# An expert layer's second product turned from channels on partitions to tokens on partitions

## The chip, the cores and the metric

The program runs on one core of a Trainium2 chip, as one launch. The metric is the device time of one execution in microseconds, the median of several runs. A core has five engines that run side by side, each with its own in-order instruction stream: TensorE (PE, with its weight loads shown apart as PEld), VectorE (DVE), ScalarE (ACT), GpSimd (POOL) and SyncE (SP), which in this kernel issues all the DMAs. They wait for one another through semaphores.

## The reference

Three layers follow one another: a linear attention, a mixture of four experts in which every token goes through all four, and a gated feed-forward layer. Only the middle one is touched by the change. With 2304 tokens, 512 channels, four experts and 1024 hidden units each:

```python
p = domain_probs / (domain_probs.sum(-1, keepdims=True) + 1e-09)   # (2304, 4)
out = np.zeros((N, D))
for e in range(E):
    h = np.maximum(x @ w1[e], 0.0)          # (2304, 1024)
    out += p[:, e:e + 1] * (h @ w2[e])      # (2304, 512)
```

The layer after it computes `((x @ w1) * (x @ w2)) @ w3 @ w_out`. All is in float32.

## The kernel before, in words

**Tiling.** The tokens are cut into six blocks j of 384 (TB). The hidden units are cut into quarters of 256, so the experts have 16 chunks c (four experts, four quarters each); the last layer has four chunks more. `visits` lists which chunk is computed for which blocks: the first visits, on the early blocks, run while the attention of later heads is still going on; the last visit (number 22, chunk 15) goes over all six blocks.

**Precision.** A float32 value x is written as hi + lo, where hi is rounded to a format that TensorE reads in one pass (F32R). A product is then three matmuls, hi·hi, hi·lo and lo·hi (`PASSES`). Some of the attention's matmuls (kvp, num and P of some head pairs) take plain float32 operands; each of them appears in the trace as two records.

**One step (visit v, block j) of the experts.** `up` (L655) makes two PSUM tiles [128 hidden units, 384 tokens], 12 matmuls each. For each of the two, DVE applies relu and multiplies by the token's share of this expert (L738; the share is the tile pb, a row of pT in DRAM broadcast over 128 partitions by a DMA, L669), ACT rounds the result to h's hi half (L741), and DVE subtracts to get the lo half (L743). One step later `down1` (L689) multiplies h by the second weight w_b. It puts channels on the partitions: for each of four groups d of 128 channels, w_b is the stationary operand, h the moving one, 384 columns wide, six matmuls. DVE adds the result to the block's running sum acc (L697 copies for the first chunk, L700 adds). At chunk 15 DVE adds into PSUM (L705), and the sum, which has its channels on partitions as the next layer wants it, is rounded and split straight into that layer's input x (L708 on ACT, L710 on DVE).

**Shares.** `load_probs` (L367 to L381) loads the 4 × 2304 shares as pn in runs of 18 floats, normalizes them on DVE, and stores them to pT.

**Order.** Nothing is written in program order. The body of the kernel lists operations with a length and a priority; `Prog.run` simulates a list scheduler with these lengths and emits each engine's instructions in the order that it finds. Expert steps have a base priority of EXPERTS·n; the tables AHEAD and KLEAD set where the attention's 16 head pairs stand among them. So a change of one operation's length, or of which engine it needs, can move instructions anywhere behind it. The PSUM pool mma has three buffers and serves `down1`; mmb has five and serves `up` once the attention is over.

**Start.** GpSimd fills the two vx tiles with constants (L826, L827) and then runs partition_all_reduce on the attention's q side (tile M from Ps, L504), 64 times. DVE subtracts M from Ps (L507), ACT takes exponentials of it (Eq, L512), and PE multiplies (num, L528). DVE, ACT and PE also work on the k side (P, mx, E, kvp).

## Time and profile before

| | us |
|---|---|
| median of three runs | 1367.98 (1367.87 to 1369.09) |
| the profiled execution, own time | 1359.98 |
| its span (first to last instruction) | 1358.2 |
| PE busy | 1336.0 (98%) |
| DVE busy | 882.3 (65%) |
| ACT busy | 439.1 (32%) |
| POOL busy | 88.5 (7%) |

The profiled execution took 1.8 us more than its span, and 8.0 us less than the median of the runs without a profile. A difference worked out inside the span is carried to the median as it is. The span has two stages: the attention, mixed with the first expert steps, up to 294 us (where the last num matmul starts), and after that the experts and the last layer alone.

In the views, busy time counts an instruction from its start to its modelled end; matmuls overlap one another, so that the pace of a row of matmuls is read from the distance between two starts, and not from the duration of one.

### The profile page before, as it was taken

The page shows a single profiled execution, that of the slowest core. Times are in us where ns is not written, and L with a number is a line of the kernel's source. Part 1 is how long each engine was busy: PE and PEld are TensorE (multiplying, and loading weights), DVE is VectorE, ACT ScalarE, POOL GpSimd, SP SyncE. Part 2 cuts the span into 40 slices and gives each one's busy share as a digit, 9 for nine tenths or more (in the row PEclk, how much of TensorE's full clock was granted, in tenths as well). Part 3 has the DMA queues.
Part 4 walks back from the last instruction along what each step waited for, and adds up shares of the span by engine and source line. Part 5 has one row for each costly group of instructions (what it writes and reads, how often), then busy time and mean ns, then how long its engine had stood idle before and what let it go on. Part 6 is the DMA issues. An engine that isn't in the chain of part 4 may idle for free.

```text
span 1358.2 us, 19233 instructions
## 1 busy us (share of the span) xinstructions
PE 1336.0 (98%) x7691; PEld 1288.8 (95%) x7691; DVE 882.3 (65%) x1553; ACT 439.1 (32%) x935; POOL 88.5 (7%) x72
## 2 busy tenths in 40 slices
PE   8899999999999999999999999999999999999998
PEld 7779989999999999999999999999999999999998
DVE  6778998888986655656656566565578737353333
ACT  6777775862322111112112121121134312121111
POOL 3333321310000000000000000000000000000000
PEclk9989999999999999999999999999999999999999
DMA  5463332223321102122021021110010202000012
GB/s 151 132 183 106 89 108 76 71 58 111 114 97 56 47 1 70 38 63 76 2 69 39 32 88 49 39 57 21 24 47 32 78 1 70 1 0 1 1 47 93
DMA packets 59640, 82.86 MB, mean 61 GB/s; under 512 B 30336, under 2 KB 33792, under 8 KB 56992
## 3 DMA queue, kind: packets, MB, share of 16 engines
q1 hardware_dynamic: 59552, 81.64, 19.7%
q8 instruction: 60, 0.98, 0.3%
q14 instruction: 28, 0.23, 0.1%
HBM read 74.63 MB, written 7.00 MB: 60 GB/s over the span
## 4 chain that ended last, share of the span: by engine, by line
PE 91%; DVE 4%; DMA 2%; ACT 2%; issue 1%; SPq 0%
PE dn L689 28%; PE up L655 28%; PE upva L655 7%; PE upvb L655 7%; PE dnv L792 7%; PE kvp L441 5%; PE psw L588 3%; PE num L528 2%; DMA d<-den 1%; PE P L414 1%; DMA den<-xq 1%; ACT E L433 1%; ACT Eq L512 0%; DVE Ps L507 0%; DVE rb L557 0%
## 5 line engine op out<-in xcount | busy, mean ns | idle before, releaser
L689 PE MATMUL dn<-h,w_b 128*128 128x384 f32 x2304 | 424.1, 335 | 1.8 <-DVE acc L697 0.9
L655 PE MATMUL up<-x,w_a 128*128 128x384 f32 x2304 | 420.3, 334 | 0.0
L689 PEld LDWEIGHTS dn<-h,w_b 128*128 128x128 f32 x2304 | 401.1, 188 | 6.5 <-DVE h L743 1.5
L655 PEld LDWEIGHTS up<-x,w_a 128*128 128x128 f32 x2304 | 401.3, 188 | 2.9
L700 DVE TENSOR_TENSOR acc<-dn,acc 128x384 f32<-128x384 f32 x336 | 185.2, 555 | 106.2 <-PE dn L689 105.1
L741 ACT CAST h<-up 128x384 fp32r<-128x384 f32 x192 | 92.1, 480 | 471.0 <-DVE up L738 467.6
L738 DVE SCALAR_TENSOR_TENSOR up<-up,pb 128x384 f32<-128x384 f32 x192 | 108.2, 563 | 110.4 <-PE up L655 109.3
L743 DVE TENSOR_TENSOR h<-up,h 128x384 fp32r<-128x384 f32 x192 | 105.5, 551 | 37.8 <-ACT h L741 37.6
L655 PE MATMUL upva<-x,w_va 128*128 128x384 f32 x576 | 108.8, 336 | 0.0
L655 PE MATMUL upvb<-x,w_vb 128*128 128x384 f32 x576 | 107.8, 336 | 0.0
L655 PEld LDWEIGHTS upva<-x,w_va 128*128 128x128 f32 x576 | 102.0, 188 | 1.7
L792 PE MATMUL dnv<-w_vo,gs 128*128 128x512 f32 x432 | 102.5, 391 | 0.0
L655 PEld LDWEIGHTS upvb<-x,w_vb 128*128 128x128 f32 x576 | 100.5, 188 | 0.0
L768 DVE TENSOR_TENSOR g<-upvb,a 128x384 f32<-128x384 f32 x48 | 26.7, 556 | 112.9 <-PE upvb L655 112.9
L504 POOL PARTITION_ALL_REDUCE M<-Ps x64 | 86.7, 1356 | 197.6 <-ACT Ps L501 187.3
L792 PEld LDWEIGHTS dnv<-w_vo,gs 128*128 128x128 f32 x432 | 80.9, 188 | 15.9
L441 PEld LDWEIGHTS kvp<-vx,E 128*128 128x128 f32 x640 | 78.6, 193 | 3.6 <-ACT E L433 1.1
L441 PE MATMUL kvp<-vx,E 128*128 128x66 f32 x640 | 78.0, 273 | 0.9 <-ACT E L433 0.8
L528 PE MATMUL num<-Eq,KV 128*128 128x288 f32 x328 | 69.9, 343 | 7.7 <-ACT Eq L512 4.0
L528 PEld LDWEIGHTS num<-Eq,KV 128*128 128x128 f32 x328 | 50.9, 190 | 15.6 <-ACT Eq L512 5.3
L763 ACT COPY a<-upva 128x384 f32<-128x384 f32 x48 | 23.0, 480 | 123.7 <-PE upva L655 123.7
L588 PE MATMUL psw<-w_f,w_f 128*128 128x512 f32 x192 | 54.6, 393 | 0.0
(92 smaller groups left out, 1055.7 us busy)
## 6 DMA issues: line engine op xcount, KB each, us to landing
raw_a<-w SPq DMA_DIRECT2D x42, 256.0 KB
raw_b<-w SPq DMA_DIRECT2D x42, 256.0 KB
qr<-qT SPq DMA_DIRECT2D x32, 288.0 KB
cr_f<-w3T SPq DMA_DIRECT2D x8, 1024.0 KB
vx<-vt SPq DMA_DIRECT2D x16, 320.0 KB
kr<-kT SPq DMA_DIRECT2D x15, 320.0 KB
rb<-rd SPq DMA_DIRECT2D x32, 144.0 KB
pb<-pT SPq DMA_DIRECT2D x24, 192.0 KB
```

The costliest lines, as they stand in the source:

```text
L441: nc.tensor.matmul(kvp()[:, a, h], E()[:, t, a, h], w()[:, t0 + t, h], start=t0 + t == 0 and h == 0 and a == 0, stop=t0 + t == 4, skip_gro ...
L504: op(POOL, 1171, lambda M=M, Ps=Ps: nc.gpsimd.partition_all_reduce(M(), Ps(), channels=128, reduce_op=bass_isa.ReduceOp.absmax), reads=[Ps ...
L528: nc.tensor.matmul(num(), KV[i]()[:, a, 2 * h:2 * h + 2].rearrange("p c d -> p (c d)"), EE[j]()[:, a], start=n == 0, stop=n == len(parts) - 1)
L588: nc.tensor.matmul(ps(), w3[fc]()[:, a, gc * 128:(gc + 1) * 128], wo[gc // 2]()[:, b, gc % 2 * DM:(gc % 2 + 1) * DM], start=gc == 0 and n ...
L655: nc.tensor.matmul(ps(), w()[:, a, kk * QF + fc * 128:kk * QF + (fc + 1) * 128], xs[b]()[:, kk], start=kk == 0 and n == 0, stop=kk == 3 an ...
L689: nc.tensor.matmul(ps(), w()[:, x, fc * DM + d * 128:fc * DM + (d + 1) * 128], hs[fc]()[:, y], start=fc == 0 and n == 0, stop=fc == 1 and ...
L700: op(DVE, dve(TB), lambda ps=ps, part=part: nc.vector.tensor_tensor(out=part(), in0=ps(), in1=part(), op=ALU.add), reads=[ps], writes=[a])
L738: op(DVE, dve(TB), lambda ps=ps, s=s: nc.vector.scalar_tensor_tensor(out=ps(), in0=ps(), scalar=0.0, in1=s(), op0=ALU.max, op1=ALU.mult), ...
L741: op(ACT, act(TB, False), lambda ps=ps, h=h: nc.scalar.copy(out=h()[:, 0], in_=ps()), reads=[ps], fills=[h])
L743: op(DVE, dve(TB), lambda ps=ps, h=h: nc.vector.tensor_tensor(out=h()[:, 1], in0=ps(), in1=h()[:, 0].bitcast(F32), op=ALU.subtract), reads ...
L768: op(DVE, dve(TB), lambda a=a, pb=pb, g=g: nc.vector.tensor_tensor(out=g(), in0=pb(), in1=a(), op=ALU.mult), reads=[a, pb], writes=[g])
L792: nc.tensor.matmul(ps(), gs[fc]()[:, a, t * 128:(t + 1) * 128], w()[:, b, fc * DM:(fc + 1) * DM], start=fc == 0 and n == 0, stop=fc == 1 a ...
```

## The change

- `down1` puts tokens on the partitions: for each of three groups t of 128 tokens, h is the stationary operand and w_b the moving one, 512 columns wide, six matmuls. Per step that is 18 matmuls of 512 columns in place of 24 of 384.
- The token's share is now one number per partition. It is applied where the sum is formed: at chunk 0 by a tensor_scalar multiply, at all later chunks by one scalar_tensor_tensor (product times share plus acc).
- Relu moves to ACT: ACT writes h's hi half with the Relu function; DVE's lo half becomes max(up, 0) − hi in one instruction. The DVE instruction L738 is gone.
- The shares are no longer stored and broadcast: the store to pT and the 24 DMAs that fill pb are gone. pn is loaded token by token, in runs of 4 floats.
- At chunk 15 the block's sum, now with tokens on partitions, is turned by 12 TensorE transposes of 128×128 float32 (three into each of four PSUM tiles tr), and then rounded and split as before. In the compiled program a transpose is one weight load and one matmul, and the program has 72 of each for the six blocks.
- The transposes need an identity matrix, eye, which GpSimd builds at the start.

```diff
-        layout = lambda t: t.rearrange("e (p c) -> p e c", p=128)
-        dma(lambda: nc.sync.dma_start(out=pn(), in_=layout(probs)), 40000, writes=[pn], after=after)
+        dma(lambda: nc.sync.dma_start(out=pn(), in_=probs.rearrange("(g p) e -> p g e", p=128)), 200000,
+            writes=[pn], after=after)
...
-        dma(lambda: nc.sync.dma_start(out=layout(pT()), in_=pn()), 40000, reads=[pn], writes=[pT])
...
-        for d in range(4):
-            ps, aft = psum(TB, f"dn{nm}", "down")
+        for t in range(3):
+            ps, aft = psum(DM, f"dn{v}_{j}_{t}", "down")
...
-                            ps(), w()[:, x, fc * DM + d * 128:fc * DM + (d + 1) * 128], hs[fc]()[:, y],
+                            ps(), hs[fc]()[:, x, t * 128:(t + 1) * 128], w()[:, y, fc * DM:(fc + 1) * DM],
...
-            elif c < NE * NQ - 1:
-                op(DVE, dve(TB), lambda ps=ps, part=part: nc.vector.tensor_tensor(
-                    out=part(), in0=ps(), in1=part(), op=ALU.add
-                ), reads=[ps], writes=[a])
-            else:
-                hi, lo = xtiles(1, j)
-                op(DVE, dve(TB), lambda ps=ps, part=part: nc.vector.tensor_tensor(
-                    out=ps(), in0=ps(), in1=part(), op=ALU.add
-                ), reads=[a], writes=[ps])
+            else:
+                op(DVE, dve(DM), lambda ps=ps, part=part, share=share: nc.vector.scalar_tensor_tensor(
+                    out=part(), in0=ps(), scalar=share(), in1=part(), op0=ALU.mult, op1=ALU.add
+                ), reads=[ps, pn], writes=[a])
+            work()
+        if c == NE * NQ - 1:
+            hi, lo = xtiles(1, j)
+            for d in range(4):
+                ps, aft = psum(TB, f"tr{j}_{d}", "up")
+                def turn(ps=ps, d=d):
+                    for t in range(3):
+                        nc.tensor.transpose(
+                            ps()[:, t * 128:(t + 1) * 128], a()[:, t, d * 128:(d + 1) * 128], eye()
+                        )
+                op(PE, 330, turn, reads=[a, eye], writes=[ps], after=aft)
...
-                    op(DVE, dve(TB), lambda ps=ps, s=s: nc.vector.scalar_tensor_tensor(
-                        out=ps(), in0=ps(), scalar=0.0, in1=s(), op0=ALU.max, op1=ALU.mult
-                    ), reads=[s], writes=[ps])
-                    op(ACT, act(TB, False), lambda ps=ps, h=h: nc.scalar.copy(out=h()[:, 0], in_=ps()),
-                       reads=[ps], fills=[h])
-                    op(DVE, dve(TB), lambda ps=ps, h=h: nc.vector.tensor_tensor(
-                        out=h()[:, 1], in0=ps(), in1=h()[:, 0].bitcast(F32), op=ALU.subtract
+                    op(ACT, act(TB, False), lambda ps=ps, h=h: nc.scalar.activation(
+                        out=h()[:, 0], in_=ps(), func=AF.Relu
+                    ), reads=[ps], fills=[h])
+                    op(DVE, dve(TB), lambda ps=ps, h=h: nc.vector.scalar_tensor_tensor(
+                        out=h()[:, 1], in0=ps(), scalar=0.0, in1=h()[:, 0].bitcast(F32),
+                        op0=ALU.max, op1=ALU.subtract,
...
+    op(POOL, 1000, lambda: make_identity(nc, eye()), writes=[eye])
```

Three places of the new order matter below. The first is GpSimd's queue at the start. An ISA row without operands is a reload of GpSimd's code library; one with M as its output is a partition_all_reduce. Before:

```order
L826 MEMSET vx_97 128x660
L826 MEMSET vx_117 128x660
L827 MEMSET vx_97 64x132
L827 MEMSET vx_117 64x132
L504 ISA
L504 ISA M_00_177<-Ps_00_172 128x288
```

After:

```order
L821 MEMSET vx_94 128x660
L821 MEMSET vx_114 128x660
L822 MEMSET vx_94 64x132
masks.py:197 MEMSET eye 128x128
masks.py:199 ISA
masks.py:199 AFFINE_SELECT eye<-eye 128x128
L822 MEMSET vx_114 64x132
L501 ISA
L501 ISA M_00_179<-Ps_00_174 128x288
```

Ahead of the first all-reduce there now stand two library reloads in place of one, with the affine_select that builds eye between them, and the second vx tile's last memset has moved behind the affine_select.

The second place is PE's queue in the last expert visit, around the end of block 0's sum; dn22_0_3 is the product of visit 22, block 0, group 3, and up22_2_0 the first product of block 2. Before:

```order
L689 MATMUL dn22_0_2_9765<-h22_0_0_9659,w_b20_9296 128x384 x3
L689 MATMUL dn22_0_2_9765<-h22_0_1_9681,w_b20_9296 128x384 x3
L655 MATMUL up22_2_0_9778<-x0_0_2_1216,w_a20_9180 128x384
...
L655 MATMUL up22_2_0_9778<-x0_0_2_1216,w_a20_9180 128x384
L689 MATMUL dn22_0_3_9797<-h22_0_0_9659,w_b20_9296 128x384 x3
```

After:

```order
L675 MATMUL dn22_0_2_8815<-w_b20_8406,h22_0_0_8717 128x512 x3
L675 MATMUL dn22_0_2_8815<-w_b20_8406,h22_0_1_8729 128x512 x3
L675 MATMUL dn22_1_0_8824<-w_b20_8406,h22_1_0_8788 128x512 x3
L675 MATMUL dn22_1_0_8824<-w_b20_8406,h22_1_1_8800 128x512 x3
L699 MATMUL tr0_0_8833<-eye_122,acc0_1486 128x128 x3
L699 MATMUL tr0_1_8837<-eye_122,acc0_1486 128x128 x3
L699 MATMUL tr0_2_8844<-eye_122,acc0_1486 128x128 x3
L699 MATMUL tr0_3_8849<-eye_122,acc0_1486 128x128 x3
L655 MATMUL up22_2_0_8856<-x0_0_2_1182,w_a20_8309 128x384
```

The operand named first is the moving one, so eye moves and acc is the weight of a transpose. The twelve transposes of a block stand behind one group of six matmuls of the next block (behind two for block 4, behind two groups and a gate for block 5).

The third place is SP's queue at the end of head pair 2, when the shares and the first expert weights are loaded. Before:

```order
L475 DMA qr_0_762<-qT 128x576
L381 DMA pT<-pn 128x4x18
L475 DMA qr_1_772<-qT 128x576
L287 DMA raw_b_512_787<-w 128x512
L537 DMA den_731<-xq_704 1x576
L669 DMA pb_0_802<-pT 128x384
L287 DMA raw_a_0_807<-w 128x512
L669 DMA pb_1_816<-pT 128x384
L669 DMA pb_2_821<-pT 128x384
L541 DMA d_3_826<-den_731 128x9
```

After:

```order
L548 DMA rb_760<-rd_725 64x576 x2
L472 DMA qr_1_770<-qT 128x576
L287 DMA raw_b_512_787<-w 128x512
L534 DMA den_731<-xq_706 1x576
L287 DMA raw_a_0_802<-w 128x512
L287 DMA raw_a_512_807<-w 128x512
L538 DMA d_3_819<-den_731 128x9
```

Between the store den and the load d of head pair 3 there stand now two weight loads, where one weight load and three broadcasts of shares stood; pT is gone.

## Rows read from the trace of the kernel before

**Rows 1.** The page: busy us, share of the span and instructions of each engine.
```profile
PE 1336.0 (98%) x7691; PEld 1288.8 (95%) x7691; DVE 882.3 (65%) x1553; ACT 439.1 (32%) x935; POOL 88.5 (7%) x72
```

**Rows 2.** Windows: stretch, length; busy (instructions) PE, PEld, DVE, ACT, POOL; clock, DMA, GB/s.
```profile
100.00:300.00 200.00, 192.83 (x1304) 186.66 (x1303) 175.28 (x334) 142.93 (x347) 54.08 (x40) 1.00 0.31 86
```

**Rows 3.** Timeline of PE, second stage: start us, us, instructions merged (xcount).
```profile
515.82 0.85 PE L588 MATMUL psw<-w_f,w_f 128*128 128x512 f32 x3
516.52 1.20 PE L689 MATMUL dn<-h,w_b 128*128 128x384 f32 x6
...
529.00 4.32 PE L655 MATMUL up<-x,w_a 128*128 128x384 f32 x24
533.16 4.32 PE L689 MATMUL dn<-h,w_b 128*128 128x384 f32 x24
```

**Rows 4.** The same view, last layer: matmuls of 512 columns.
```profile
1071.27 4.28 PE L792 MATMUL dnv<-w_vo,gs 128*128 128x512 f32 x18
1075.38 2.27 PE L655 MATMUL upva<-x,w_va 128*128 128x384 f32 x12
```

**Rows 5.** The same view, attention: kvp in plain float32, P in three passes.
```profile
242.02 1.89 PE L441 MATMUL kvp<-vx,E 128*128 128x66 f32 x16
243.72 1.05 PE L528 MATMUL num<-Eq,KV 128*128 128x288 f32 x6
...
249.35 0.88 PE L414 MATMUL P<-wb,kh 128*128 128x256 f32 x6
250.07 1.00 PE L441 MATMUL kvp<-vx,E 128*128 128x66 f32 x8
```

**Rows 6.** Groups by line: xcount | busy us, mean ns of one | idle before, releaser.
```profile
L700 DVE TENSOR_TENSOR acc<-dn,acc 128x384 f32<-128x384 f32 x336 | 185.2, 555 | 106.2 <-PE dn L689 105.1
L738 DVE SCALAR_TENSOR_TENSOR up<-up,pb 128x384 f32<-128x384 f32 x192 | 108.2, 563 | 110.4 <-PE up L655 109.3
L804 DVE TENSOR_TENSOR oacc<-dnv,oacc 128x512 f32<-128x512 f32 x54 | 37.1, 688 | 19.0 <-PE dnv L792 19.0
```

**Rows 7.** Waits of PE's weight loads, 90 to 300 us: total us, times, longest.
```profile
PEld num L528 <- ACT xq L533: 3.2, 5, 0.7
...
PEld dn L689 <- DVE h L743: 1.5, 3, 0.9
PEld dn L689 <- DVE acc L697: 1.2, 1, 1.2
...
PEld num L528 <- DVE Eq L520: 1.0, 2, 0.6
...
PEld dn L689 <- DVE acc L700: 0.6, 1, 0.6
```

**Rows 8.** The start: timelines of POOL, ACT and PE, and a DMA of the chain.
```profile
2.01 0.35 POOL L827 MEMSET vx<- 64x132 f32 x2
9.72 1.24 POOL L504 PARTITION_ALL_REDUCE M<-Ps  x1 [7.36 <-ACT Ps L501]
...
13.05 0.66 ACT L433 ACTIVATE E<-P 128x256 f32<-128x256 f32 x2 [0.23 <-PE kvp L441]
...
14.93 1.00 PE L441 MATMUL kvp<-vx,E 128*128 128x66 f32 x8
...
3.05 4.52 DMA vx<-vt
```

**Rows 9.** Instructions of line 504: duration ns min/median/max, first and last start.
```profile
L504 POOLq MODIFY_POOL_CONFIG  x2: 4/4/4, 2.4 to 2.4; - x2
```

**Rows 10.** Windows (columns as in Rows 2) and timeline around 57 and 72 us.
```profile
56.00:58.00 2.00, 0.49 (x3) 0.31 (x3) 1.94 (x6) 1.59 (x5) 1.27 (x1) 1.00 1.04 194
58.00:60.00 2.00, 1.77 (x9) 1.28 (x8) 2.00 (x5) 2.00 (x6) 1.52 (x2) 1.00 0.87 310
...
72.16 2.08 PE L414 MATMUL P<-wbd,kr 128*128 128x256 f32 x4 [1.94 <-ACT E L433]
...
74.00:76.00 2.00, 2.00 (x11) 1.97 (x10) 1.05 (x3) 0.71 (x2) 1.05 (x1) 0.50 0.85 249
```

More of the change, by code (lines that the diff above doesn't have):

```diff
@@ L8 @@
 from concourse._compat import with_exitstack
+from concourse.masks import make_identity
 F32 = mybir.dt.float32
@@ L200, in fused_kernel @@
     pools["ring2"] = ec(tc.tile_pool(name="ring2", bufs=2))
-    pools["pb"] = ec(tc.tile_pool(name="pb", bufs=6))
     pools["stage"] = ec(tc.tile_pool(name="stage", bufs=3))
@@ L228, in fused_kernel @@
     wb2 = keep([128, 2, 2 * FEAT], F32R, "wb2", "at")
-    pn = keep([128, NE, NTILE], F32, "pn")
+    pn = keep([128, NTILE, NE], F32, "pn")
     psm = keep([128, NTILE], F32, "psm")
-    pT = keep([NE, NT], F32, "pT", "dram")
+    eye = keep([128, 128], F32, "eye")
     wfold = [keep([128, 2, DM], F32, f"wfold{i}", "dram") for i in range(4)]
@@ L661, in up @@
         return ps
-    acc, weight = {}, {}
-    def share(e, j):
-        if weight.get(j, (None,))[0] != e:
-            t = V("pb", [128, TB], F32, "pb", 6, f"pb{e}_{j}")
-            dma(lambda: nc.sync.dma_start(
-                out=t(), in_=pT()[e:e + 1, j * TB:(j + 1) * TB].to_broadcast([128, TB])
-            ), 1 << 18, reads=[pT], writes=[t])
-            weight[j] = e, t
-        return weight[j][1]
+    acc = {}
     def down1(v, j, hs):
@@ L696, in down1 @@
+            part = lambda t=t: a()[:, t]
+            share = lambda t=t: pn()[:, j * 3 + t, c // NQ:c // NQ + 1]
             if c == 0:
-                op(DVE, dve(TB), lambda ps=ps, part=part: nc.vector.tensor_copy(out=part(), in_=ps()), reads=[ps],
-                   fills=[a], after=[] if j < 3 else start["C"])
-            elif c < NE * NQ - 1:
-                op(DVE, dve(TB), lambda ps=ps, part=part: nc.vector.tensor_tensor(
-                    out=part(), in0=ps(), in1=part(), op=ALU.add
-                ), reads=[ps], writes=[a])
-            else:
-                hi, lo = xtiles(1, j)
-                op(DVE, dve(TB), lambda ps=ps, part=part: nc.vector.tensor_tensor(
-                    out=ps(), in0=ps(), in1=part(), op=ALU.add
-                ), reads=[a], writes=[ps])
-                op(ACT, act(TB, False), lambda d=d, ps=ps, hi=hi: nc.scalar.copy(out=hi()[:, d], in_=ps()),
+                op(DVE, dve(DM), lambda ps=ps, part=part, share=share: nc.vector.tensor_scalar(
+                    out=part(), in0=ps(), scalar1=share(), scalar2=None, op0=ALU.mult
+                ), reads=[ps, pn], fills=[a], after=[] if j < 3 else start["C"])
+            else:
+                op(DVE, dve(DM), lambda ps=ps, part=part, share=share: nc.vector.scalar_tensor_tensor(
+                    out=part(), in0=ps(), scalar=share(), in1=part(), op0=ALU.mult, op1=ALU.add
+                ), reads=[ps, pn], writes=[a])
@@ new lines, in down1 @@
+            work()
[9 more added lines that the diff above has]
+                op(PE, 330, turn, reads=[a, eye], writes=[ps], after=aft)
+                op(ACT, act(TB, False), lambda d=d, ps=ps: nc.scalar.copy(out=hi()[:, d], in_=ps()),
@@ L709, in down1 @@
                    reads=[ps], fills=[hi])
-                op(DVE, dve(TB), lambda d=d, ps=ps, hi=hi, lo=lo: nc.vector.tensor_tensor(
+                op(DVE, dve(TB), lambda d=d, ps=ps: nc.vector.tensor_tensor(
                     out=lo()[:, d], in0=ps(), in1=hi()[:, d].bitcast(F32), op=ALU.subtract
                 ), reads=[ps, hi], fills=[lo])
-            work()
+                work()
     def experts():
@@ L733, in experts @@
                 pg.base = EXPERTS * n
-                hs, s = [], share(c // NQ, j)
+                hs = []
                 for fc in range(2):
@@ L782, in down2 @@
         if c == 0:
-            oacc[j] = V("acca" if j < 3 else "accb", [128, 4 * TB], F32, "acc", 3, f"oacc{j}")
+            oacc[j] = V("acca" if j < 3 else "accb", [128, 3 * DM], F32, "acc", 3, f"oacc{j}")
         o = oacc[j]
```

16 lines of the change are left out of this document (6 added, 10 removed).

## The prediction

> **What bounds the kernel now.** I read the page first: PE is busy 98% of the span [rows 1]. A busy PE need not be a fast one, so the second view is the timeline of PE in the second stage. There 24 matmuls of 384 columns start at 529.00 and the next group at 533.16 [rows 3], which is 173.3 ns for each, with no idle time named anywhere in the row; this goes on to the end. In that stage (294 us to the end, about 1,060 us) only the number and the pace of PE's instructions count, and DVE's time is free. The third view is the windows of the first stage: from 100 to 300 us PE is busy 192.83 of 200 us and DVE 175.28 [rows 2]. So here DVE is nearly full, PE does wait, and DVE's time can matter. The fourth view is the list of what PE's weight loads waited for from 90 to 300 us: eight entries, 12.4 us in all, from 3.2 us (ACT's xq) to 0.6 us (DVE's acc) [rows 7]. The fifth is GpSimd's queue at the very start [rows 8, 9].
>
> **Term 1, the second product.** 16 chunks times 6 blocks are 96 steps. Before, a step is 24 matmuls of 384 columns, 4.16 us [rows 3]. After, it is 18 of 512. The nearest row is dnv, which has the new shape exactly (tokens stationary, weights moving, groups of six): 18 start at 1071.27 and the next at 1075.38, 4.11 us or 228 ns each [rows 4]. That saves 0.05 us a step, **-4.8 us**. For the ends: P in three passes takes (250.07 - 249.35)/6 = 120 ns at 256 columns [rows 5] and up 173.3 at 384, so the straight line gives 226.7 at 512, 4.08 us a step, -7.7 us; the other 512-column product, psw, takes 0.70/3 = 233 ns [rows 3], 4.20 us a step, +3.8 us. I take dnv because operands and group length are the same. The matmul count falls by a quarter, but the columns streamed (9,216 a step) do not, and that is why so little comes of it.
>
> **Term 2, the transposes.** 72 are added, all on PE in the dense stage, where nothing hides them. No row shows a transpose. Lower bound: the straight line of term 1 at 128 columns, 66.7 ns, 4.8 us in all. Upper bound: a whole plain float32 product. Such a product is two records; 16 records of kvp take 243.72 - 242.02 = 1.70 us [rows 5], 106 ns a record, 213 ns for two, 15.3 us in all. Between them: kvp moves only 66 columns and still takes 106 ns a record, so its float32 weight load of 128 columns looks like what sets the pace. A transpose has one such load (of acc) and one matmul. I take one kvp record, 106 ns: **+7.7 us**, 4.8 to 15.3.
>
> **Term 3, waits in front of the transposes.** They need the sum of the block's third group; DVE needs about 0.69 us for one (L804 has the same shape [rows 6]), and the order puts six matmuls, 1.37 us, between. So the wait is normally covered. DVE is also converting the next layer's weights at that time, so a late sum is possible: the row for PE waiting on acc is 1.2 us once [rows 7]. One of the six sets meeting that gives **+1.2 us**; bounds 0 and 6 × 1.2 = 7.2.
>
> **Term 4, the start.** Before, GpSimd's last memset ends at 2.36 us, the library reload is issued at 2.4 [rows 9], and the first all-reduce starts at 9.72, when its operand comes from ACT [rows 8]: the 7.36 us in between hide the reload, whatever it takes. After, two reloads stand in the queue. With L for a reload, the eye memset and the first three others end near 2.4, then L, the affine_select (0.2 to 1.24 us by the memset and the all-reduce [rows 8]; I take 0.7), the last memset 0.2, and L again: the first all-reduce starts at 3.3 + 2L. L is at most 7.3 us. The row nearest to it is the load of vx in the same microseconds, 4.52 us to landing [rows 8]. I take the middle of these two, 5.9: the all-reduce starts at 15.1, 5.4 us late. Behind it in DVE's queue stand the last k-side steps of head pair 0, and for them PE's kvp group at 14.93 waits; its E was ready at 13.05 + 0.66 = 13.71 [rows 8], so 1.2 us of the delay is absorbed: **+4.2 us**. PE idles only 7.2 us from 100 to 300 us [rows 2], so little gives this back. Bounds: nothing, if L is 3.2 us or less, to 7.0 us with L = 7.3. On top of that comes the clock: after PE's wait of 1.94 us at 72.16 the granted clock in 74 to 76 us was 0.50, that is 1.2 GHz [rows 10]; a few microseconds at half pace cost up to 3 us more, so the upper end is 10. vx's second DMA and two q loads are held in SP's queue by the late memset, but DVE and ACT are standing then anyway. The Trainium skill, GPSIMD Engine Reference, Instruction dispatch, says that a freshly loaded kernel pays about 6 us (5.95) at its first call, unseen in the profile; by that the all-reduce would start at 15.2, this term would be +4.3 and the sum +4.1. No row of this trace shows that figure, only that it is hidden here.
>
> **Term 5, DVE and ACT in the first stage.** L738 goes: 24 of its 192 executions stand in front of the attention's last DVE instruction, at 0.563 us [rows 6], 13.5 us of DVE time. The sums stay about level: 3 × 0.69 against 4 × 0.555 us a step [rows 6]. The h chain loses one link of three. ACT keeps its one instruction per h, now Relu; no second activation table load stands in ACT's order. What this can return to PE is what PE waits for: the entries that name DVE are 1.5 + 1.2 + 1.0 + 0.6 = 4.3 us [rows 7]. I take them: **-4.3 us**. The ends are -12.4, if all eight entries hang on DVE's backlog, and +3.2, since the list scheduler finds a new order and a wait as long as the largest entry may appear. In the second stage DVE loses 95 us more, and that brings nothing, since PE does not wait there.
>
> **Term 6, the DMAs.** pT (512 runs of 72 bytes) and 24 broadcasts of 192 KB go; pn becomes 2304 runs of 16 bytes. From 58 to 60 us the engines moved 310 GB/s at a share of 0.87, 356 at full; from 56 to 58 us, with pn among the transfers, 194 at 1.04 [rows 10]. 388 KB should take 1.1 us and took 2, so pn's 512 runs cost 0.9 us, and 2304 would cost 4: 3 us more in front of rd and rb of head pair 2. Against that, pT's 0.9 us and 1.2 MB of broadcasts, 3.3 us, go from the same 15 us. The two about cancel on the path: **0**, with 3 us either way.
>
> **The sum.** -4.8 + 7.7 + 1.2 + 4.2 - 4.3 + 0 = +4.0 us on the profiled execution's 1359.98 us. The runs without a profile have a median of 1367.98, 8.0 us more; the difference is carried over: **1372.0 us**, 0.3% slower.
>
> **The rivals.** (a) *The transposes pay for a whole float32 product*, 213 ns each: +7.6 more, 1379.6. For it: plain float32 is paid twice everywhere in this trace. Against it: the compiled program has one record for each. The Trainium skill, TensorE: Matmul & The Clock Gate, Part 4, tells of about 275 ns for a transpose within a kernel. That would make 19.8 us of the 72, and 1384.1; no row here shows it. Chance 0.12, the page's figure included.
> (b) *Not slower: the second reload is hidden.* The place is GpSimd's queue ahead of the first all-reduce, the price the 4.2 us of term 4, and the point from which it decides is L = 3.2 us, or a first reload that costs nothing. Then the sum is -0.2 us, 1367.8. For it: the trace shows only that a reload fits into 7.36 us. Chance 0.25, within 2.7 us.
> (c) *Faster: the first stage is bound by DVE altogether.* Then relief of 13.5 us returns all 12.4 us of waits and the late start is partly caught up: 4.0 - 8.1 = -4.1, 1363.9, and 1361.0 with transposes at 66.7 ns. For it: DVE is busy 175 of 200 us. Against it: most entries name ACT, and ACT gains nothing. Chance 0.21.
> (d) *The relief brings nothing*, since PE's order is fixed and ACT's chains are as long as before: 1376.3. It lies in the forecast's own range.
>
> **How the numbers follow.** The forecast with (d) has a chance of 0.42 and runs from +2.8 to +9.5 us, 1370.8 to 1377.5. About 0.2% (2.7 us) is what a measurement of this kernel can tell from no change. Slower is the forecast and (a), 0.54; same is (b), 0.25; faster is (c), 0.21. The range takes in (b), most of (c) and most of (a): 1362 to 1381.
>
> **What would show it.** Right: dn groups of 18 at 4.11 us; tr records at about 106 ns; the first all-reduce near 15 us with a second MODIFY_POOL_CONFIG ahead of it; PE idle for several microseconds before 20 us; fewer waits of PE from 100 to 300 us. Wrong: an all-reduce still at about 9.7 us (term 4 falls); a dense stage that shrinks or grows by other than 4 us (terms 1 to 3); a first stage that ends well before 290 us (term 5 too small).

## The result: slower by 0.7%

| | before | after |
|---|---|---|
| median, us | 1367.38 (10 runs) | 1374.85 (10 runs) |
| ratio, 95% interval | | 1.0072 (1.0048 to 1.0095) |
| profiled execution: own time / span, us | 1359.98 / 1358.2 | 1384.07 / 1382.3 |

The forecast was 1372.0 with a range of 1362 to 1381. By the ratio the change costs 9.8 us, by the medians 7.5. The runs of the changed kernel fall into two groups, seven at 1373.6 to 1378.9 and three at 1383.1 to 1384.5, and the profiled one is of the upper group, so that its 24.1 us over the profile of before are more than the change usually costs; its rows show mechanisms, the medians show prices. The profiled execution of before is not a usual one either: at 1359.98 us it is faster than each of the 115 other executions of that kernel on record here (the fastest of them took 1360.16).

The page of the changed kernel: busy time by engine, and the granted clock in 40 slices.

```profile
PE 1352.2 (98%) x7187; PEld 1232.5 (89%) x7187; DVE 793.7 (57%) x1265; ACT 440.8 (32%) x935; POOL 88.6 (6%) x74
...
PEclk9989899999999999999999999999999999999999
```

DVE's busy time is 89 us less than in [rows 1], and PE won nothing by it: it is still busy 98%. The clock row has an 8 in its third and fifth slice, 69 to 104 and 138 to 173 us.

The second stage first. Timeline of PE, changed kernel: start us, us, instructions merged.

```profile
545.97 4.35 PE L652 MATMUL up<-x,w_a 128*128 128x384 f32 x24
550.16 4.28 PE L675 MATMUL dn<-w_b,h 128*128 128x512 f32 x18
554.28 4.35 PE L652 MATMUL up<-x,w_a 128*128 128x384 f32 x24
...
1034.68 1.47 PE L699 MATMUL tr<-eye,acc 128*128 128x128 f32 x12
1035.90 4.43 PE L652 MATMUL up<-x,w_a 128*128 128x384 f32 x24
1040.17 1.08 PE L675 MATMUL dn<-w_b,h 128*128 128x512 f32 x4
```

The 18 matmuls of dn take 554.28 - 550.16 = 4.12 us, where [rows 3] answers with 4.16 for 24. But up now takes 4.19 behind them (4.16 before). A whole step is 8.31 us after and 8.32 before. Twelve transposes take 1035.90 - 1034.68 = 1.22 us, 102 ns each, and the up behind them 4.27 us, 0.08 more than elsewhere. PE waits for nothing from 300 us to the end: the view of its waits is empty there.

Where the second stage begins, the last matmul of num tells (xcount: duration ns min/median/max, first and last start from 270 us on). Before, then after:

```profile
L528 PE MATMUL num<-Eq,KV x48: 289/295/379, 270.7 to 293.9; 128*128 128x288 f32 x48
L525 PE MATMUL num<-Eq,KV x72: 289/295/401, 270.1 to 316.0; 128*128 128x288 f32 x72
```

From there to the end it is 1358.2 - 293.9 = 1064.3 us before and 1382.3 - 316.0 = 1066.3 after. The second stage grew by 2.0 us, and one of the 96 steps' dn, 4.1 us of work, had moved ahead of it. The other 22 us of the 24.1 lie in the first stage.

Groups by line of the changed kernel (xcount | busy us, mean ns of one | idle before, releaser):

```profile
L688 DVE SCALAR_TENSOR_TENSOR acc<-dn,pn,acc 128x512 f32<-128x512 f32 x270 | 201.9, 749 | 106.0 <-PE dn L675 105.2
L737 DVE SCALAR_TENSOR_TENSOR h<-up,h 128x384 fp32r<-128x384 f32 x192 | 106.3, 555 | 193.7 <-ACT h L734 192.9
L734 ACT ACTIVATE h<-up 128x384 fp32r<-128x384 f32 x192 | 94.3, 493 | 459.3 <-PE up L652 458.6 <-DVE w_b L275 0.7
```

The sum with the share in it is 749 ns, not the 688 of the plain addition of the same shape [rows 6].

The start. GpSimd's timeline, changed kernel:

```profile
10.52 0.28 POOL masks.py:199 TENSOR_SCALAR_AFFINE_SELECT eye<-eye 128x128 f32<-128x128 f32 x1 [8.04 <-issue]
...
17.42 2.50 POOL L501 PARTITION_ALL_REDUCE M<-Ps  x2 [6.35 <-issue]
```

GpSimd's queue at line 501 (duration ns min/median/max, first and last start):

```profile
L501 POOLq MODIFY_POOL_CONFIG  x2: 4/4/4, 11.3 to 11.3; - x2
```

PE's timeline:

```profile
21.51 1.95 PE L438 MATMUL kvp<-vx,E 128*128 128x66 f32 x8 [5.66 <-ACT E L430]
...
28.87 1.90 PE L438 MATMUL kvp<-vx,E 128*128 128x66 f32 x16
```

Two reloads stand one behind the other: GpSimd is idle for 8.04 us at the first and for 6.35 us at the second, whose MODIFY_POOL_CONFIG is issued at 11.3. The first all-reduce starts at 17.42 (9.72 in [rows 8]). PE idles 5.66 us, and it was at half clock afterwards: kvp x8 takes 1.95 us where [rows 8] has 1.00. The group of 16 kvp products that starts here at 28.87 started at 20.42 before, 8.45 us earlier. PE's timeline, kernel before:

```profile
20.42 1.90 PE L441 MATMUL kvp<-vx,E 128*128 128x66 f32 x16
```

More of the loss in this execution lies in two later stretches. Windows of the changed kernel (columns as in [rows 2]: the third number from the right is the clock):

```profile
80.00:84.00 4.00, 3.20 (x11) 2.84 (x12) 2.56 (x8) 3.56 (x10) 1.24 (x1) 0.52 0.02 1
84.00:88.00 4.00, 3.73 (x11) 2.72 (x11) 3.42 (x7) 1.80 (x5) 1.24 (x1) 0.50 0.50 122
...
160.00:164.00 4.00, 4.00 (x20) 4.00 (x20) 3.27 (x7) 1.13 (x3) 1.25 (x1) 0.50 0.24 77
```

From 80 to 96 us and from 156 to 172 us the clock is at its lower level, 1.2 GHz, for most of the time; in the profiled execution of before, that was so only from 72 to 80 us:

```profile
72.00:76.00 4.00, 3.84 (x14) 3.48 (x15) 1.73 (x5) 2.71 (x8) 1.24 (x1) 0.50 0.90 275
76.00:80.00 4.00, 3.91 (x17) 2.79 (x17) 3.97 (x10) 2.78 (x7) 1.24 (x1) 0.67 0.49 128
```

A window of 4 us at clock c loses 4 (1 - c) where PE has work. Summed over the windows of the two stretches that is 13.7 us; the one stretch before lost 3.3. These 10.4 us and the 8.45 of the start are 18.8 of the 22.1 us by which the attention's last product is later (316.0 against 293.9).

### The profile page after: what moved, and what is told of

Same layout as the page of the kernel before. It is cut to its first block, busy times and chain, and to the rows that moved or that the text cites. A ratio compares the mean times of both kernels' runs of the same rounds, so it can differ in the third digit from the quotient of the medians.

```text
span 1382.3 us, 17874 instructions
## 1 busy us (share of the span) xinstructions
PE 1352.2 (98%) x7187; PEld 1232.5 (89%) x7187; DVE 793.7 (57%) x1265; ACT 440.8 (32%) x935; POOL 88.6 (6%) x74
## 4 chain that ended last, share of the span: by engine, by line
PE 91%; DVE 4%; DMA 3%; issue 1%; ACT 1%; POOL 0%; SPq 0%; POOLq 0%; DVEq 0%; ACTq 0%
PE up L652 28%; PE dn L675 27%; PE upva L652 7%; PE upvb L652 7%; PE dnv L787 7%; PE kvp L438 5%; PE psw L585 3%; PE num L525 3%; PE P L411 2%; DMA rb<-rd 1%; DVE rb L554 1%; DMA rd<-d 1%; PE tr L699 1%; DVE mx L421 1%; DVE Ps L504 0%
## 5 line engine op out<-in xcount | busy, mean ns | idle before, releaser
L675 PE MATMUL dn<-w_b,h 128*128 128x512 f32 x1728 | 417.5, 392 | 0.6 <-DVE h L737 0.6
L675 PEld LDWEIGHTS dn<-w_b,h 128*128 128x128 f32 x1728 | 322.0, 188 | 65.6 <-DVE h L737 1.0
L688 DVE SCALAR_TENSOR_TENSOR acc<-dn,pn,acc 128x512 f32<-128x512 f32 x270 | 201.9, 749 | 106.0 <-PE dn L675 105.2
L734 ACT ACTIVATE h<-up 128x384 fp32r<-128x384 f32 x192 | 94.3, 493 | 459.3 <-PE up L652 458.6
L737 DVE SCALAR_TENSOR_TENSOR h<-up,h 128x384 fp32r<-128x384 f32 x192 | 106.3, 555 | 193.7 <-ACT h L734 192.9
L438 PEld LDWEIGHTS kvp<-vx,E 128*128 128x128 f32 x640 | 84.3, 206 | 9.0 <-issue 7.1
L438 PE MATMUL kvp<-vx,E 128*128 128x66 f32 x640 | 83.4, 285 | 6.3 <-ACT E L430 5.7
L525 PE MATMUL num<-Eq,KV 128*128 128x288 f32 x328 | 72.9, 354 | 8.1 <-ACT Eq L509 4.4
L509 ACT ACTIVATE Eq<-Ps 128x288 f32<-128x288 f32 x128 | 51.3, 446 | 11.5 <-DVE Ps L504 11.3
```

The lines of the kernel that those rows point to most:

```text
L438: nc.tensor.matmul(kvp()[:, a, h], E()[:, t, a, h], w()[:, t0 + t, h], start=t0 + t == 0 and h == 0 and a == 0, stop=t0 + t == 4, skip_gro ...
L509: op(ACT, act(HS), lambda a=a, E=E, Ps=Ps: nc.scalar.activation(out=E()[:, a], in_=Ps(), func=AF.Exp, scale=1.0 - 2 * a), reads=[Ps], fill ...
L525: nc.tensor.matmul(num(), KV[i]()[:, a, 2 * h:2 * h + 2].rearrange("p c d -> p (c d)"), EE[j]()[:, a], start=n == 0, stop=n == len(parts) - 1)
L675: nc.tensor.matmul(ps(), hs[fc]()[:, x, t * 128:(t + 1) * 128], w()[:, y, fc * DM:(fc + 1) * DM], start=fc == 0 and n == 0, stop=fc == 1 a ...
L688: op(DVE, dve(DM), lambda ps=ps, part=part, share=share: nc.vector.scalar_tensor_tensor(out=part(), in0=ps(), scalar=share(), in1=part(), ...
L734: op(ACT, act(TB, False), lambda ps=ps, h=h: nc.scalar.activation(out=h()[:, 0], in_=ps(), func=AF.Relu), reads=[ps], fills=[h])
```

## The experiments

All ratios are to the kernel before, run beside each kernel; 0.001 is 1.37 us, and the difference of two ratios is uncertain by about 0.003, 4 us. "Lost to the clock" is an estimate: the span times what the mean granted clock lacks to 1, as the mean over all runs of a kernel; "rest" is the mean span without it. It counts time at the lower clock as lost also where PE had no work. Differences of these two columns are good to 1 or 2 us. The row of before is of the runs beside e1 to e4; in the later ones its rest was 1353.7 to 1354.0 and its loss 11.8 to 12.4.

| run | what differs | median us | ratio (95%) | lost to the clock, us | rest, us |
|---|---|---|---|---|---|
| before | | 1367.57 | 1 | 11.4 | 1354.4 |
| after | | 1374.85 | 1.0072 (1.0048 to 1.0095) | 15.1 | 1360.7 |
| e1 | after, identity built late | 1376.32 | 1.0070 (1.0045 to 1.0094) | 16.1 | 1358.0 |
| e2 | after, shares in long runs, planner told 40000 | 1369.71 | 1.0026 (1.0005 to 1.0046) | 9.2 | 1358.7 |
| e3 | e1 and e2 together | 1360.92 | 0.9955 (0.9932 to 0.9978) | 4.2 | 1355.8 |
| e4 | before, identity built at the start | 1373.10 | 1.0042 (1.0020 to 1.0064) | 14.4 | 1356.8 |
| e5 | e3 without transposes | 1355.88 | 0.9903 (0.9881 to 0.9925) | 6.4 | 1347.4 |
| e6 | e3, transposes twice (planner told twice the length) | 1368.14 | 1.0000 (0.9982 to 1.0018) | 3.8 | 1364.0 |
| e7 | before, shares in long runs | 1363.83 | 0.9971 (0.9950 to 0.9992) | 9.2 | 1353.4 |
| e8 | e3, relu on DVE | 1365.85 | 0.9979 (0.9962 to 0.9997) | 6.6 | 1356.8 |
| e9 | e3 with short runs (order of e3) | 1362.97 | 0.9964 (0.9940 to 0.9989) | 6.4 | 1355.2 |
| e10 | e3 with the planner told 200000 | 1373.13 | 1.0039 (1.0015 to 1.0063) | 14.0 | 1357.6 |
| e11 | e1, one idle gap of PE filled | 1369.22 | 1.0015 (0.9992 to 1.0037) | 9.0 | 1359.4 |
| e12 | e3, three idle gaps filled | 1361.11 | 0.9953 (0.9934 to 0.9971) | 3.4 | 1355.5 |

### e1, e2, e3, e4: the start and the load of the shares

e1 moves the identity behind the attention:

```
-    op(POOL, 1000, lambda: make_identity(nc, eye()), writes=[eye])
...
-    start["C"] = [op("HOST", 1, phase_c, after=pg.ops[f1:])]
+    attention = pg.ops[f1:]
+    start["C"] = [op("HOST", 1, phase_c, after=attention)]
+    op(POOL, 1000, lambda: make_identity(nc, eye()), writes=[eye], after=attention)
```

> The identity is built after the attention's last instruction instead of at the start; nothing else differs from the changed kernel. Theory (start): the identity's affine_select makes GpSimd load a second library, all-reduces begin at 17.4 us instead of 9.7, the products that build kvp x16 begin at 28.9 us instead of 20.4, and those 8.4 us are the loss. Then the first all-reduce is back at about 9.7 us, kvp x16 at about 20.4, and the time is 1374.9 - 8.4 = 1366.5 us, ratio to the kernel before 0.999. Rival (first stage): the lateness is made good later on by shorter waits, and the loss is in the half-clock stretches at 80-92 and 158-172 us that the other order and the shares' load bring; then the all-reduces are early too but the time stays at 1371 to 1375 us, ratio 1.003 to 1.005.

e2 lays the shares out on the host, so that a partition reads one run:

```
-        dma(lambda: nc.sync.dma_start(out=pn(), in_=probs.rearrange("(g p) e -> p g e", p=128)), 200000,
+        dma(lambda: nc.sync.dma_start(out=pn(), in_=probs.rearrange("p (g e) -> p g e", e=NE)), 40000,
...
-        "probs": np.ascontiguousarray(moe_domain_probs),
+        "probs": lay(moe_domain_probs, (NTILE, 128, NE), (1, 0, 2), (128, NTILE * NE)),
```

> The changed kernel with the shares laid out beforehand so that each partition reads one run of 288 bytes (128 runs) instead of 18 runs of 16 bytes (2304 runs). Theory (start): the shares' load is beside the path, no change: 1374.9 us, ratio 1.005. Rival (the load's small runs): they delay raw_a, raw_b and above all rb (landed 5.2 us after its issue at 72.1 us), DVE and then TensorE wait, and the clock is halved at 80 to 92 us; without them the rb transfer takes some 2 us, the half-clock stretch at 80-92 goes, and the time falls by 4 to 7 us: 1368 to 1371 us, ratio 1.000 to 1.003.

e3 has both edits.

> Both edits: identity late and shares in long runs. Theory (start): as with the identity late alone, 1366.5 us, ratio 0.999. Rival (small runs add to it): 1360 to 1363 us, ratio 0.995 to 0.997. If neither matters: 1374.9 us.

e4 adds the identity to the kernel before, behind the memsets of vx, and nobody reads it:

```
+    eye = keep([128, 128], F32, "eye")
...
+    op(POOL, 1000, lambda: make_identity(nc, eye()), writes=[eye])
```

> The kernel before, with the same identity built at the same place of the program and read by nobody. Theory (start): the second library alone delays the all-reduces to about 17.4 us and the time rises by 8.4 us less what is absorbed: 1373 to 1376 us, ratio 1.004 to 1.006. Rival (the lateness is made good, the loss comes from the rest of the change): 1367 to 1370 us, ratio 1.000 to 1.002.

In e1 the all-reduce is back at 9.47 us and the group of kvp follows, as the theory of the start wants; the time did not move (0.3 us by the ratios). e4 against before, and e2 against e3, differ in the order of GpSimd's queue and in no other, so these pairs price the identity alone. They say that the identity at the start costs 5.7 (e4) and 9.7 us (e3 to e2). The edit on the shares is worth 15.8 us with an early start (e1 to e3) and 6.3 us with a late one (after to e2). Neither theory as written holds: both causes are real, and their prices do not add. The time of e2 is the one that its rival named, but its profile does not bear the rival's mechanism out: the clock is still down at 80 to 88 us (0.64 and 0.51). GpSimd's timeline of e4:

```profile
17.80 2.50 POOL L506 PARTITION_ALL_REDUCE M<-Ps  x2 [6.71 <-issue]
```

PE's timeline of e1 shows where the late part of its loss begins, and the windows what follows:

```profile
69.94 0.40 PE L493 MATMUL Pq<-q,wst 128*128 128x288 f32 x1 [1.06 <-ACT Ps L498]
72.49 2.07 PE L411 MATMUL P<-wbd,kr 128*128 128x256 f32 x4 [2.01 <-DVE x L562]
...
143.96 0.40 PE L493 MATMUL Pq<-q,wst 128*128 128x288 f32 x1 [1.75 <-ACT Ps L498]
...
148.43 0.41 PE L493 MATMUL Pq<-q,wst 128*128 128x288 f32 x1 [1.46 <-DVE q L484]
```

```profile
72.00:76.00 4.00, 3.51 (x13) 3.15 (x13) 2.25 (x7) 3.26 (x9) 1.24 (x1) 0.50 0.02 1
76.00:80.00 4.00, 3.73 (x10) 2.63 (x10) 3.73 (x7) 2.11 (x6) 1.24 (x1) 0.50 0.61 142
80.00:84.00 4.00, 4.00 (x19) 3.86 (x18) 3.81 (x7) 1.90 (x5) 0.00 (x0) 0.50 0.81 242
```

Waits of one to two microseconds are followed by a clock of 0.50, for some 14 us each time in e1 (some 7 in before, some 20 in the later stretch of e10 and e11). The windows from 16 to 320 us lose 13.6 us in e1 that way, 6.8 in e2, 10.2 in e4 and nothing in e3. Take these away from the spans, and the profiled executions of the four are at 1359.4, 1362.5, 1359.5 and 1355.9 us in place of 1373.0, 1369.3, 1369.7 and 1355.9: most of what tells them apart is clock.

### e9, e10: runs of 16 bytes, or the number that the planner is told

e2 changed two things in one line, the runs and the 40000 in place of 200000, the load's size as the planner, the kernel's list scheduler, is told. e9 is e1 with only 200000 changed to 40000; e10 is e3 with only 40000 changed to 200000.

> Identity late, the shares read in 2304 runs of 16 bytes as in the changed kernel, but the planner is told the short load's 40000 instead of 200000, so every engine issues in the order of the kernel with both edits. Theory (transfer): the small runs themselves hold up rb, raw_a and raw_b, TensorE waits at about 70 to 72 us and its clock is halved: 1370 to 1376 us, ratio 1.002 to 1.006. Rival (order): the loss of the kernel with the early all-reduces came from the other order that the planner's 200000 brings (waits of 1.75 and 1.46 us on Pq at 144 and 148 us, half clock at 148 to 164): 1360 to 1365 us, ratio 0.995 to 0.998.

> The other half: identity late, the shares in 128 runs of 288 bytes, but the planner is told 200000, so the engines issue in the order of the kernel whose identity alone was moved. Theory (transfer): 1360 to 1364 us, ratio 0.995 to 0.997. Rival (order): 1370 to 1376 us with half clock at 148 to 164 us, ratio 1.002 to 1.006. If both count, each of the two lies in between, at 1364 to 1370 us.

The number decides: it costs 11.5 us with long runs (e3 to e10) and 14.5 with short ones (e9 to e1). The 2304 short runs cost 1.2 us with one number (e3 to e9) and 4.2 with the other (e10 to e1), neither clearly more than the uncertainty. PE, DVE and ACT issue in the same order in e1 and e10, and in e3 and e9, so the rivals of both expectations were right. Of the number's price some 10 us are clock and 2 or 3 are rest. With 200000 the planner takes the shares as later and moves their normalization by an instruction or two, and from there on the list scheduler builds another order. DVE's instructions around the rb of head pair 2, with 40000 (e9) and with 200000 (e1):

```
e9: 92 L376 TENSOR_TENSOR pn<-pn,psm 128x72
    93 L275 TENSOR_TENSOR w_a_767<-raw_a_0_691,w_a_767 128x512
    94 L275 TENSOR_TENSOR w_a_767<-raw_a_512_696,w_a_767 128x512
    95 L554 TENSOR_TENSOR rb_742<-xq_541,rb_742 64x576 x2
e1: 92 L376 TENSOR_TENSOR pn<-pn,psm 128x72
    93 L275 TENSOR_TENSOR w_a_767<-raw_a_0_691,w_a_767 128x512
    94 L275 TENSOR_TENSOR w_a_767<-raw_a_512_696,w_a_767 128x512
    95 L275 TENSOR_TENSOR w_b_780<-raw_b_0_703,w_b_780 128x512
    96 L554 TENSOR_TENSOR rb_755<-xq_541,rb_755 64x576 x2
```

With 200000 a weight split, wanted only by the experts, comes ahead of rb. The long waits at Pq come with this order, long runs or short. PE's timeline and a window of e10:

```profile
147.88 0.40 PE L493 MATMUL Pq<-q,wst 128*128 128x288 f32 x1 [1.75 <-ACT Ps L498]
```

```profile
152.00:156.00 4.00, 2.98 (x9) 2.46 (x10) 3.94 (x7) 3.65 (x9) 0.26 (x1) 0.50 0.56 181
```

It is the same 1.75 us as in e1; e3 and e9 have no wait of over 1.1 us at that place and keep the clock there. The wait at 72 us does not come with the order: e3 has it too, 1.87 us long, and keeps its clock in its profiled execution, while e8 with the same 1.87 us at that place loses it, and runs the same four products in 2.08 us. PE's timeline of e3:

```profile
72.18 1.13 PE L411 MATMUL P<-wbd,kr 128*128 128x256 f32 x4 [1.87 <-ACT E L430]
```

### e11, e12: is it the idle time of PE that costs the clock?

e11 puts eight products of zeros behind one product of e1, in the gap ahead of 72.49; the order of all else stays.

```
...
+    FILL = {'Pq4_10': 8}
+    def filled(nm, fn):
+        def run():
+            fn()
+            n = FILL.get(nm, 0)
+            if n:
+                ps = pools["mma"].tile([128, 512], F32, tag="mm", bufs=3, name=f"fill_{nm}")
+                for _ in range(n):
+                    nc.tensor.matmul(ps, zf()[:, :128], zf(), start=True, stop=True)
+        return run
...
```

> The kernel with only the identity moved (1376 us, half clock at 72 to 84 and 148 to 164 us in its profile), with eight products of zeros (128x512, bf16) issued behind Pq of pair 4, head 1, first half, where TensorE waits 2.01 us at 70.5 to 72.5 us; the order of everything else is the same and nothing reads the zeros' sum. Theory (the clock falls because TensorE stands idle there): the stretch at 72 to 88 us keeps its clock and the time falls by what it lost, 4 x (0.50 + 0.50 + 0.50 + 0.21) = 6.8 us: 1369 to 1371 us, ratio 1.001 to 1.003. Rival (the clock falls for another reason, or the half clock there is no loss because TensorE waits anyway): 1375 to 1378 us, ratio 1.006 to 1.008.

PE's timeline and windows of e11 at the filled place (one of the eight has no record), and the window of its start:

```profile
75.89 1.67 PE L356 MATMUL fill_Pq<-zf 128*128 128x512 bf16 x7
77.40 1.03 PE L426 MATMUL P<-wbd,kr 128*128 128x256 f32 x4
```

```profile
76.00:80.00 4.00, 3.58 (x21) 2.52 (x19) 3.30 (x10) 3.94 (x12) 1.90 (x2) 1.00 0.02 1
80.00:84.00 4.00, 3.89 (x25) 3.52 (x26) 3.91 (x8) 3.50 (x9) 1.24 (x1) 1.00 0.85 198
...
0.00:20.00 20.00, 17.13 (x61) 13.02 (x62) 9.85 (x25) 8.58 (x20) 5.50 (x11) 0.76 0.56 159
```

P x4 takes 1.03 us (2.07 in e1), the clock stays at 1.00, and the median falls by 7.1 us (7.5 by the ratios) where 6.8 was expected. The added products are work that nobody needs, and they save time. So the idle gap costs the clock, and the clock costs the time: against e1 the loss to the clock is 7.1 us less, and the rest is not less. The profiled execution by itself does not show the gain. It is the slowest of its twelve, 1376.34 us, since it ran at half clock from 10 to 20 us, which e1's did not, and the unfilled stretch kept its half clock, from 144 to 164 us.

e12 fills three gaps of e3:

```
+    FILL = {'Pq3_10': 6, 'num3_01': 4, 'Pq4_10': 8}
```

> The kernel with both edits (1360.9 us; its profiled execution kept the full clock throughout, 1355.9 us of span, but others of it are 1 to 7 us longer), with products of zeros in three gaps of TensorE: six behind Pq of pair 3, head 1, first half (a wait of 1.50 us at 56.2), four behind num of pair 3, head 0, second half (1.01 us at 60.7), eight behind Pq of pair 4, head 1, first half (1.87 us at 70.3). Each filling is shorter than its gap. Theory (idle gaps of TensorE cost clock in some executions): the median comes down to what the undisturbed execution took, 1355.9 + 1.8 = 1357.7 us, ratio 0.992 to 0.994, and the spread shrinks. Rival (the spread has another cause): 1360 to 1362 us, ratio 0.995 to 0.997.

Nothing gained (0.3 us by the ratios): the rival was right. The executions of e3 that are longer than its profiled one do not, on the whole, lose their time in these three gaps. Where they do, no trace here shows. A candidate is the start: e5, e10 and e11 have a stretch of some 10 us at half clock there, worth 5 us, which e3 and e12 do not have in their profiled executions, and six runs of e12 stand at 1357.3 to 1359.6 us and six at 1362.6 to 1363.4. Whether a given gap costs the clock also differs between executions: e3 and e9 come to this product of num with the same waits, 1.50 and 1.49 us, and then part. First PE's timeline of e3, then of e9:

```profile
57.74 1.24 PE L525 MATMUL num<-Eq,KV 128*128 128x288 f32 x4 [1.50 <-ACT Eq L509]
...
59.47 1.24 PE L525 MATMUL num<-Eq,KV 128*128 128x288 f32 x4 [0.23 <-ACT xq L530]
61.72 1.24 PE L525 MATMUL num<-Eq,KV 128*128 128x288 f32 x4 [1.01 <-ACT Eq L509]
```

```profile
57.81 1.24 PE L525 MATMUL num<-Eq,KV 128*128 128x288 f32 x4 [1.49 <-ACT Eq L509]
...
59.53 2.16 PE L525 MATMUL num<-Eq,KV 128*128 128x288 f32 x4 [0.23 <-ACT xq L530]
62.53 2.29 PE L525 MATMUL num<-Eq,KV 128*128 128x288 f32 x4 [0.83 <-ACT Eq L509]
```

### e5, e6: the transposes

e5 takes them out of e3, and hi and lo read the sum as it lies:

```
-                        nc.tensor.transpose(
-                            ps()[:, t * 128:(t + 1) * 128], a()[:, t, d * 128:(d + 1) * 128], eye()
-                        )
...
+                part = lambda d=d: a().rearrange("p t m -> p (t m)")[:, d * TB:(d + 1) * TB]
```

e6 issues each of e3's twice:

```
-                    for t in range(3):
+                    for t in (0, 1, 2) * 2:
...
-                op(PE, 330, turn, reads=[a, eye], writes=[ps], after=aft)
+                op(PE, 660, turn, reads=[a, eye], writes=[ps], after=aft)
```

> The kernel with the identity late and the shares in long runs, without its 72 transposes: the sums go to the next stage as they lie, so the values of the output are others. It tells what the transposes cost. At the pace read from the changed kernel's trace (12 in 1.22 us, and the next up 24 takes 4.27 us instead of 4.18) they cost 72 x 0.102 + 6 x 0.09 = 7.9 us: 1360.9 - 7.9 = 1353.0 us, ratio to the kernel before 0.989. Rival one (each works alone, 213 ns): 15.3 us, 1345.6 us, ratio 0.984. Rival two (a wait stands at the same place without them): 1358 to 1361 us, ratio 0.993 to 0.995.

> The same kernel with every transpose issued twice (144 instead of 72). By the trace's pace 1360.9 + 7.3 = 1368.2 us, ratio to the kernel before 1.000; by 213 ns each 1376.2 us, ratio 1.006; hidden beside other work 1360.9 us, ratio 0.9955.

By the ratios 72 transposes cost 7.1 us (e5 to e3) and 72 more 6.2 us (e3 to e6), each uncertain by some 4 us. The profiles say it more sharply, since in the second stage the granted clock is 1.00 and PE waits for nothing in all three. The last matmul of num in e3, e5 and e6:

```profile
L525 PE MATMUL num<-Eq,KV x36: 289/295/378, 270.2 to 291.8; 128*128 128x288 f32 x36
L525 PE MATMUL num<-Eq,KV x48: 289/295/378, 269.8 to 296.5; 128*128 128x288 f32 x48
L525 PE MATMUL num<-Eq,KV x37: 289/295/378, 269.8 to 293.7; 128*128 128x288 f32 x37
```

From there to the end of their spans (1355.9, 1352.8 and 1365.7 us) it is 1064.1, 1056.3 and 1072.0 us, with the same work in it but for the transposes: 7.8 us for the first 72, 7.9 for the second. Timeline of PE in e6:

```profile
1010.21 2.78 PE L699 MATMUL tr<-eye,acc 128*128 128x128 f32 x24
1012.75 4.43 PE L652 MATMUL up<-x,w_a 128*128 128x384 f32 x24
```

24 take 2.54 us, 106 ns each. A float32 transpose is paid once (one record, and its spacing is that of one record of kvp), and nothing hides it.

### e7, e8: the old load of the shares, and relu

e7 is the kernel before with its shares laid out for one run of 288 bytes per partition:

```
-        dma(lambda: nc.sync.dma_start(out=pn(), in_=layout(probs)), 40000, writes=[pn], after=after)
+        dma(lambda: nc.sync.dma_start(
+            out=pn(), in_=probs.rearrange("p (e c) -> p e c", e=NE)
+        ), 40000, writes=[pn], after=after)
...
-        "probs": np.ascontiguousarray(moe_domain_probs.T),
+        "probs": lay(moe_domain_probs, (128, NTILE, NE), (0, 2, 1), (128, NE * NTILE)),
```

e8 is e3 with the maximum back on DVE:

```
-                    op(ACT, act(TB, False), lambda ps=ps, h=h: nc.scalar.activation(
-                        out=h()[:, 0], in_=ps(), func=AF.Relu
+                    op(DVE, dve(TB), lambda ps=ps: nc.vector.tensor_scalar(
+                        out=ps(), in0=ps(), scalar1=0.0, scalar2=None, op0=ALU.max
+                    ), writes=[ps])
+                    op(ACT, act(TB, False), lambda ps=ps, h=h: nc.scalar.copy(out=h()[:, 0], in_=ps()),
...
```

> The kernel before with its shares read in 128 runs of 288 bytes instead of 512 runs of 72 bytes, and nothing else. Theory (transfers): the load is also in its way, the half-clock stretch at 72 to 80 us goes, which is worth 0.50 x 4 + 0.33 x 4 = 3.3 us: 1364.3 us, ratio 0.9976, and the rest of the way to 1360.9 us comes from the other product. Rival (the change's lighter VectorE ends the stretch): no change, 1367.6 us, ratio 1.000.

> The kernel with the identity late and the shares in long runs, with relu back on VectorE (a maximum in place, then the copy on ScalarE and the subtraction): one VectorE instruction of some 480 to 690 ns more for each half of h, 192 in all. Theory (relief counts in the first stage): slower by 2 to 6 us, 1363 to 1367 us, ratio 0.997 to 0.9995. Rival (VectorE has room, TensorE waits for chains over ScalarE and GpSimd): 1360 to 1362 us, ratio 0.995 to 0.996.

e7 gains 4.0 us, so the kernel before also paid for its 512 runs (the planner's order is not in play, its figure is 40000 in both and all engines issue alike). By which path is not shown: the interval only just excludes no change, and in e9 2304 runs cost 1.2 us. From e7 to e3, the change itself without the two side effects, it is another 2.2 us, less than its uncertainty. In e7's profile the half clock stands at other places (60 to 68 and 140 to 148 us) and shorter at the old one (76 to 80 us), and has not gone, as its theory had it. e8 is slower than e3 by 3.3 us by the ratios, about as much as that difference is uncertain; it loses more to the clock (6.6 us against 4.2). The added instruction also makes the planner give PE, DVE and ACT another order, so e8 does not price DVE's work alone: it points to relief, and does not prove it.

## Why the prediction was right, and which steps were wrong

The sign came out, and the size lies in the range (+4.0 us forecast, +9.8 measured by the ratio, 7.5 by the medians), though 9.8 is just past the +9.5 at which the forecast's own stretch ended. That the sum came so near is in part luck: term 6 alone was short by 6.3 us, more than the 5.8 by which the sum was; terms 1 and 5 promised more than came, and against them terms 3 and 4 cost less, in the change as made, than forecast.

| term | forecast us | measured us |
|---|---|---|
| 1, second product | -4.8 | about -1: 96 × (8.31 - 8.32) |
| 2, transposes | +7.7 | +7.8 (e5) and +7.9 (e6) in the second stage |
| 3, waits ahead of them | +1.2 | 0 |
| 4, the start | +4.2 (0 to 10) | +5.7 (e4), +9.7 (e3 to e2), +0.3 (e1 to after) |
| 5, relief of DVE and ACT | -4.3 | -3.3 (e8, with another order) |
| 6, the DMAs | 0 (±3) | +11.5 by the order (e10), +1.2 by the runs (e9); both with the late start +6.3 (e2 to after) |

**Term 1** fell with its silent assumption that up stays at 4.16 us. dn came within 0.01 us of dnv's 4.11, but up behind 512-column matmuls took 4.18 to 4.19 us.

**Term 2** was right in kind and size: the starts of transposes are 102 to 106 ns apart, and the time follows this spacing, so rival (a) falls. The Trainium skill, TensorE: Matmul & The Clock Gate, Part 4, has about 275 ns for a 128×128 transpose in bf16 within a kernel. A record here lasts 272 ns too, but that is not what the time follows. **Term 3**: none of the six sets waited.

**Term 4** was right in mechanism; L was taken as 5.9 and is 8.0 for the first reload, past the bound of 7.3, and some 6.3 for the second, and the group of kvp is 8.45 us late, in part by the half clock ahead of it. The Trainium skill, GPSIMD Engine Reference, Instruction dispatch, says about 6 us for the first call after a load. The second reload agrees (6.1 us from its issue at 11.3 to 17.42); the first is 2 us longer, and why is not shown. Rival (b) falls in its mechanism by this row and by e4: the reload is not hidden. Yet in the change as made taking it away gained nothing (e1).

**Term 5** can be read only from a remainder. The rest of e3, the time without the clock's loss, is 1.4 us above that of before, although its second product and transposes alone add 6.5 there; so some 5 us are gained elsewhere, near the 4.3. By the same sum e1, with the change's order, gains some 3. This is argued, not shown, and the remainder takes in whatever else the change spares, the broadcasts too. Rival (c) falls with the sign: from 100 to 300 us PE is busy 191.99 us, no more than before (192.83 [rows 2]). In the change as made, rival (d) describes what is seen: nothing of it reaches the time.

**Term 6 is the step that failed.** It weighed the DMAs as bytes and runs and set them at zero. The dearest part of that line of the diff was the argument 200000, which moves no byte on the chip and gives PE, DVE and ACT another order: 11.5 us (e3 to e10), where the runs that the term did weigh cost 1.2 (e3 to e9). Term 5's upper end allowed for a new order, "a wait as long as the largest entry may appear", 3.2 us; it did not count that such a wait takes the clock with it, although [rows 10] show just that after a wait of 1.94 us. The profile of before hid how much there was to lose or to win: it lost 3.3 us to the clock, where the usual execution of before loses 11 to 12.

**Open**: why the late start costs nothing on top of the 200000 order (e1 to after, 0.3 us) while it costs 9.7 us on top of the other. The estimate of the clock's loss narrows it down. In the rest the late start costs 2.7 us (e1 to after), 2.9 (e3 to e2) and 2.4 (before to e4), the same within its uncertainty; the loss to the clock goes by -1.0, +5.0 and +3.0 us. So it is in the clock that the prices do not add: with the 200000 order 16 us are lost to it with the early start already. Why the late start adds none to these is not shown.

e3 beats both kernels: 0.9955 (0.9932 to 0.9978), 6.2 us under the kernel before. By the two columns all of that is clock (4.2 us lost in place of 11.4); its rest is 1.4 us longer.

## What to carry to other kernels

Where a planner sets the order, read its costs in a diff as code: a cost that is changed beside a harmless edit can be worth more than the edit. Price a wait of TensorE in a half-full stage at its length plus the half-clock stretch that may come behind it, and look first at stages with room between the products, not at the engine whose busy time falls. Build constants that need another GpSimd library where nobody waits for GpSimd.
